# Scores in 64 by 64 tiles, an early fetch of sigmoid's table, and a rewritten order of all engines

## The chip, the cores and the metric

The kernel runs on one core of a Trainium2 chip. The time is device microseconds of one execution. Before the change three runs gave a median of 335.84 us (335.83 to 341.89). Inputs and weights start in device memory, and the output ends there.

## The reference

Three stages follow one another, all in float32, for a batch of 2 and 768 positions.

```python
# 1. linear attention with a decaying state: 8 heads, head_dim 48
for t in range(S):
    cur = einsum('bhd,bhe->bhde', u * k_t, v_t)
    y_t = einsum('bhd,bhde->bhe', r_t, state + cur)
    state = w_t[..., None] * state + einsum('bhd,bhe->bhde', k_t, v_t)
# x = y, heads side by side: [2, 768, 384]
# 2. gated MLP: d_ff 1024, gate over the positions
h = gelu_tanh(x @ w_in);  a, v = halves(h)
v_n = layernorm(v) * g_ln
x = x + (a * (einsum('ts,bsd->btd', w_sg, v_n) + b_sg)) @ w_out
# 3. channel mixing with a shift by one position
xk, xr = mu_k * x + (1 - mu_k) * x_prev, mu_r * x + (1 - mu_r) * x_prev
out = sigmoid(xr @ w_r) * (relu(xk @ w_k) ** 2 @ w_v)
```

## The kernel before, in words

The positions are cut into four blocks of 384, g = 0 to 3 (two for each batch entry). In the attention a block has three packs (L, q, D, j, g, d, K, f: loading and the decayed copies of r and k, VectorE work) and four units of two heads each, sixteen units in all. A unit's TensorE work is: T (turn: transposes of the keys), A (scores: keys against queries for three chunks of 128 positions), P (sums: two columns behind the scores, in the same PSUM tile), S and s (states and carry), J (inner: masked scores times values), N (inject) and I (outer: state times queries). VectorE's m (weigh, L359) masks the scores and n (now, L365) scales the values; ScalarE's k, x and O copy the turned keys, the states and the result. The fourth unit of each block is made of sixteen rows of each pack, which SyncE's queue moves with DMAs (6, and o for the way back, L396 and L397).

An operation on plain float32 operands shows as two weight loads and two matmuls in the trace; the stages behind the attention split each float32 number into a high and a low part (float32r) and add three products (`mm3`, L188 to L190). Weights come as raw words and are converted in chunks C0 to C38: l is the load, x, b, t VectorE's joining of the words, h the high part on ScalarE, o the low part on VectorE, r and q range checks on ScalarE.

The second stage runs by tiles v and u (both of `mm1`), M (`mm2`) and W (`mm_out`), the third by E (`mm_k`), R (`mm_r`) and Z (`mm_v`), with X, G, H (L490), Y, z and y as their elementwise steps and stores. E is a chain of five steps: nine matmuls on TensorE, Relu on ScalarE (L514), the square on VectorE (L516), the high part on ScalarE (L521), the low part on VectorE (L523). The tiles v, u, M, W, E and the idle matmuls share one PSUM pool of three buffers (`ps_d`); R and Z have another of five (`ps_e`). E's result kr has two buffers.

Nothing of the order is left to a scheduler: `ORDER` is a list of some 1250 tokens, each a step of the above with its number, and every engine and SyncE's DMA queue issue their own instructions in the order of this list. `E0.3` stands five times in it, once for each step of that chain. The token `e` is an idle matmul of 512 columns on zeros (L621). A step that is not ready stops its engine until it is.

The scores put the keys of head h (48 rows from row 64h) into the array with 128 columns, and write head h into the PSUM bank h:

Of the kernel before, what the change touches and what calls it, by code (L numbers as in the profile page):

```python
# [40 lines left out]
x3.2 e e T4 k4 A5 S4.0 K4 P5 s4.0 C2.b S4.1 x4.0 C2.t D5 C1.o j5 g5 J4 s4.1 C2.q x4.1 C2.h e e e N4 T5 I4 o3 o3 o3 X0.2.h X0.2.l X0.0.h f5 k5 C2.o K5
m5 C5.l v0.2 S5.0 s5.0 S5.1 J5 w6 63 L6 C5.x d5 X0.0.l n5 C3.x D6 C5.b C3.b x5.0 s5.1 C0.r x5.1 f4 X0.1.h X0.1.l C3.t j6 C5.t q6 64 65 w7 C4.l L7 v0.0
N5 T6 I5 O4 k6 S6.0 s6.0 S6.1 x6.0 v0.0 A7 P7 g6 n7 m7 s6.1 C3.h x6.1 f6 O5 C5.h C0.q v0.1 T7 d6 C5.o C4.x K6 k7 C5.r A6 P6 n6 m6 S7.0 s7.0 S7.1 J7
x7.0 s7.1 C5.q C4.b C4.t x7.1 C3.r C3.q C4.h v0.2 D7 C3.o C4.o N7 A8 P8 J6 T8 N6 u0.1 I7 q7 w8 C10.l C14.l q8 w9 n8 j7 g7 m8 K7 d7 I6 k8 v0.2 v0.0
S8.0 S8.1 O7 C14.h x8.0 C4.r J8 s8.1 S8.2 x8.1 f7 A9 P9 s8.2 L8 D8 j8 g8 n9 u0.1 v0.0 v0.0 x8.2 O6 K8 m9 d8 o7 o7 C8.l 66 67 o7 w10 q10 68 u0.3 N8
v0.1 v0.2 v0.1 T9 u0.2 k9 u0.0 I8 S9.0 S9.1 A10 X1.0.h x9.0 s9.1 S9.2 X1.2.h C10.h x9.1 u0.2 J9 P10 s9.2 X1.0.l C14.o C8.h X1.1.h f8 u0.3 O8 x9.2 m10
X1.2.l L9 D9 X1.1.l n10 C7.l C7.h C8.o v1.0 N9 v1.2 T10 A11 j9 v0.0 w11 q9 g9 d9 B L10 K9 v0.2 v0.1 v1.0 k10 S10.0 S10.1 v0.1 x10.0 v0.1 C10.o J10 P11
v0.2 n11 s10.1 S10.2 I9 x10.1 s10.2 C9.l C6.l f9 x10.2 v1.2 u0.0 O9 C7.o m11 C11.l q11 w12 v1.1 T11 N10 v1.2 v1.0 C6.h k11 C6.o D10 K10 j10 u1.1 u1.3
S11.0 S11.1 C11.h u1.3 x11.0 A12 P12 s11.1 S11.2 x11.1 v1.0 J11 s11.2 x11.2 u1.2 T12 N11 I10 I11 v1.1 69 C15.l L11 g10 m12 d10 C11.o n12 A13 v1.2 v1.0
v1.0 O10 k12 S12.0 s12.0 S12.1 v1.1 J12 x12.0 s12.1 P13 v1.2 u1.2 O11 x12.1 C9.h C9.o v1.1 C15.h v1.1 C12.l C12.h u1.1 o11 w13 C4.q D11 v1.1 v1.2  # L50
C15.o K11 C12.o n13 m13 C21.l o11 j11 g11 d11 N12 u1.0 u1.0 M0.3 M0.1 T13 k13 M0.2 A14 S13.0 s13.0 S13.1 J13 x13.0 s13.1 611 o11 X2.1.h C17.l w14
x13.1 P14 N13 T14 I13 I12 m14 n14 610 C26.l M0.2 A15 k14 C17.h C21.r C17.o O12 C21.q O13 S14.0 s14.0 S14.1 x14.0 J14 P15 s14.1 x14.1 X2.0.h M0.0 T15
C21.x m15 C16.l w15 C16.h C16.o X2.1.l M0.1 C26.x n15 C26.b C21.b M0.1 M0.0 C21.t M0.2 X2.2.h X2.2.l X2.0.l M0.3 C18.l C13.l N14 v2.1 k15 S15.0 s15.0
S15.1 C18.r x15.0 f11 J15 s15.1 N15 x15.1 I14 I15 C18.q f10 C13.h O15 v2.1 M0.3 C26.r O14 | C26.q C13.o C26.t v2.0 M1.2 C26.h C26.o M1.2 C20.l C20.r
C21.h v2.0 C19.l C21.o M0.0 v2.0 v2.2 M1.1 C20.q G0.3.h C20.x C20.b C20.t C18.x C18.b C18.t C18.h v2.0 v2.2 v2.2 v2.1 M1.1 M1.1 M1.0 M1.3 C18.o C19.x
C19.b M1.3 C19.r v2.1 C20.h v2.2 C19.t v2.0 v2.2 C19.h v2.1 C19.q M1.3 v2.0 M1.0 C19.o v2.2 M1.0 G0.2.h v2.1 u2.3 u2.0 u2.3 u2.1 u2.2 o15 C24.l G0.1.h
G0.0.h G0.1.l G0.0.l C20.o G0.2.l u2.0 u2.1 u2.2 G0.3.l W0.0 C24.x C24.b W0.0 M1.2 W0.1 W0.1 W0.2 C24.r C24.q C27.l o15 o15 C25.l C25.x X3.2.h C27.r
X3.0.h C27.q X3.0.l v3.0 C25.r X3.1.h C25.q v3.0 C25.b X3.2.l W0.2 X3.1.l C24.t v3.1 C24.h v3.0 C22.l C24.o C25.t C25.h C25.o C27.x C27.b C27.t C34.l
C23.l v3.2 u3.3 v3.0 v3.1 v3.1 u3.3 v3.2 u3.2 u3.0 u3.1 v3.2 u3.2 v3.0 v3.1 u3.0 v3.2 v3.0 C34.x C34.b C34.t v3.1 v3.1 G1.3.h v3.2 v3.2 C34.h G1.2.h
G1.2.l G1.1.h u3.1 G1.0.h C27.h C34.r C34.q C22.r C22.q M2.2 M2.2 C34.o C27.o M2.1 C23.x M2.1 C23.b C22.x G1.0.l M2.2 C22.b C22.t C23.t G1.3.l M3.3  # L60
# [838 lines left out]
```

## Time and profile before

| what | value |
|---|---|
| median of 3 runs | 335.84 us |
| profiled execution | 336.38 us, span 334.6 us |
| granted TensorE clock, mean | 0.996 |
| TensorE matmul busy | 323.1 us (97%), 2529 matmuls |
| VectorE busy | 232.0 us (69%) |
| ScalarE busy | 179.8 us (54%) |
| GpSimd busy | 35.4 us (11%) |

The profiled execution stands 0.54 us above the median of the runs, and its own time is 1.78 us longer than the span from its first to its last instruction. Busy time is an average over stages with different limits: the attention ends at about 122 us, the second stage runs mixed with it and to about 202 us, and the third from there to the end. A matmul's printed length overlaps that of the next, so that what a group of matmuls costs is read from its start to the start of the next group.

### The profile page before, as it was taken

The page shows a single profiled execution, that of the slowest core. Times are in us where ns is not written, and L with a number is a line of the kernel's source. Part 1 is how long each engine was busy: PE and PEld are TensorE (multiplying, and loading weights), DVE is VectorE, ACT ScalarE, POOL GpSimd, SP SyncE. Part 2 cuts the span into 40 slices and gives each one's busy share as a digit, 9 for nine tenths or more (in the row PEclk, how much of TensorE's full clock was granted, in tenths as well). Part 3 has the DMA queues.
Part 4 walks back from the last instruction along what each step waited for, and adds up shares of the span by engine and source line. Part 5 has one row for each costly group of instructions (what it writes and reads, how often), then busy time and mean ns, then how long its engine had stood idle before and what let it go on. Part 6 is the DMA issues. An engine that isn't in the chain of part 4 may idle for free.

```text
span 334.6 us, 6544 instructions
## 1 busy us (share of the span) xinstructions
PE 323.1 (97%) x2529; PEld 300.7 (90%) x2534; DVE 232.0 (69%) x427; ACT 179.8 (54%) x439; POOL 35.4 (11%) x78
## 2 busy tenths in 40 slices
...
GB/s 204 223 246 199 194 175 155 78 240 128 39 167 70 145 97 111 93 49 111 65 47 119 71 49 47 143 0 2 72 0 2 0 42 32 0 2 25 46 25 53
DMA packets 16500, 29.80 MB, mean 89 GB/s; under 512 B 2256, under 2 KB 12496, under 8 KB 16464
## 3 DMA queue, kind: packets, MB, share of 16 engines
...
## 4 chain that ended last, share of the span: by engine, by line
PE 77%; DVE 9%; ACT 5%; POOL 3%; DMA 2%; issue 2%; SPq 1%; ACTq 0%; POOLq 0%; DVEq 0%
PE po L542 11%; PE ps L188 5%; PE ps L190 5%; PE ps L189 5%; PE pk L188 4%; PE pk L190 4%; PE pk L189 4%; PE po L190 3%; PE po L189 3%; PE po L188 3%; PE pA L319 3%; PE py L385 2%; PE pu L188 2%; PE py L375 2%; PE pu L190 2%; PE pu L189 2%
## 5 line engine op out<-in xcount | busy, mean ns | idle before, releaser
L188 PE MATMUL pk<-xk_hi,wk_hi 128*128 128x384 f32 x96 | 32.5, 338 | 1.1 <-ACT kr L514 1.1
L188 PE MATMUL ps<-wsg,vn_hi 128*128 128x384 f32 x96 | 32.7, 340 | 0.0
L190 PE MATMUL ps<-wsg,vn_lo 128*128 128x384 f32 x96 | 32.5, 339 | 0.0
L190 PE MATMUL pk<-xk_hi,wk_lo 128*128 128x384 f32 x96 | 32.4, 337 | 0.0
L189 PE MATMUL ps<-wsg,vn_hi 128*128 128x384 f32 x96 | 32.4, 337 | 0.0
L189 PE MATMUL pk<-xk_lo,wk_hi 128*128 128x384 f32 x96 | 32.4, 337 | 0.0
L514 ACT ACTIVATE kr<-pk 128x384 f32<-128x384 f32 x32 | 15.5, 490 | 28.8 <-PE pk L190 14.6
L521 ACT CAST kk_hi<-kr 128x384 fp32r<-128x384 f32 x32 | 16.2, 512 | 19.3 <-DVE kr L516 19.3
L542 PE MATMUL po<-pl_win_hi,kk_hi 128*128 128x384 f32 x81 | 23.0, 337 | 0.0
L523 DVE TENSOR_TENSOR kk_lo<-kr,kk_hi 128x384 fp32r<-128x384 f32 x32 | 17.7, 555 | 6.9 <-ACT kk_hi L521 6.5
L359 DVE TENSOR_TENSOR am<-pA,c_sb 128x768 f32<-128x768 f32 x16 | 15.2, 951 | 8.9 <-PE pA L326 6.2
L516 DVE TENSOR_TENSOR kr<-kr 128x384 f32<-128x384 f32 x32 | 17.4, 555 | 4.4 <-ACT kr L514 4.3
L545 DVE TENSOR_TENSOR rr<-po,rr 128x384 f32<-128x384 f32 x12 | 6.6, 554 | 18.9 <-PE po L190 8.4
L188 PEld LDWEIGHTS pk<-xk_hi,wk_hi 128*128 128x128 f32 x96 | 18.0, 188 | 1.5 <-ACT kr L514 1.4
L542 PE MATMUL po<-pl_win_lo,kk_hi 128*128 128x384 f32 x63 | 18.4, 338 | 0.0
L190 PEld LDWEIGHTS ps<-wsg,vn_lo 128*128 128x128 f32 x96 | 18.0, 188 | 0.3 <-DVE vn_lo L446 0.2
L188 PEld LDWEIGHTS ps<-wsg,vn_hi 128*128 128x128 f32 x96 | 18.0, 188 | 0.3
L542 PE MATMUL po<-pl_win_hi,kk_lo 128*128 128x384 f32 x54 | 18.2, 338 | 0.0
L189 PEld LDWEIGHTS ps<-wsg,vn_hi 128*128 128x128 f32 x96 | 18.0, 188 | 0.1
L190 PEld LDWEIGHTS pk<-xk_hi,wk_lo 128*128 128x128 f32 x96 | 18.0, 188 | 0.0
L189 PEld LDWEIGHTS pk<-xk_lo,wk_hi 128*128 128x128 f32 x96 | 18.0, 188 | 0.0
L188 PE MATMUL pu<-xs_hi,win_hi 128*128 128x384 f32 x48 | 16.8, 350 | 0.1
...
## 6 DMA issues: line engine op xcount, KB each, us to landing
...
```

Source lines behind the costliest of these rows:

```text
L188: T.matmul(ps, lh, rh, start=(i == 0), stop=False)
L189: T.matmul(ps, lh, rl, start=False, stop=False)
L190: T.matmul(ps, ll, rh, start=False, stop=(i == n - 1))
L319: T.matmul(u.pA[:, h, c * C:(c + 1) * C], u.kinv[o:o + D, c, :], u.rp[o:o + D, c, :], start=True, stop=True)
L359: V.tensor_mul(u.am.rearrange("p h (c t) -> p h c t", c=NCB), u.pA[:, :, :TB].rearrange("p h (c t) -> p h c t", c=NCB), mask[:, None, None ...
L375: T.matmul(u.py[64 * h:64 * h + m, cs], u.vk[:, c, h * D:h * D + m], u.am[:, h, cs], start=(c == 0), stop=False)
L385: T.matmul(u.py[o:o + D, c * C:(c + 1) * C], u.state(c)[o:o + D, :], u.rp[o:o + D, c, :], start=False, stop=(c == NCB - 1))
L514: A.activation(kr, ps, AF.Relu)
L516: V.tensor_mul(kr, kr, kr)
L521: A.copy(hi, kr)
L523: V.tensor_sub(lo, kr, hi.bitcast(F32))
L542: T.matmul(pv[g][s], l, wv[i][r], start=st, stop=(i == KF - 1 and l is ll))
```

## The change

It makes three edits that act. A helper `minus` and the steps p and `rest` come with the diff too, but no token of the new order calls them, so they issue nothing.

```diff
         def scores(u):
             u.pA = ps_A.tile([P, 2, 512], F32, name=f"pA_{u.n}", tag="pA")
             for c in range(NCB):
-                for h in range(2):
+                for h, q in ((0, 0), (1, 64), (0, 64), (1, 0)):
                     o = 64 * h
-                    T.matmul(u.pA[:, h, c * C:(c + 1) * C], u.kinv[o:o + D, c, :], u.rp[o:o + D, c, :], start=True, stop=True)
+                    T.matmul(u.pA[q:q + 64, h, c * C:(c + 1) * C], u.kinv[o:o + D, c, q:q + 64], u.rp[o:o + D, c, :], start=True, stop=True)
...
+        elif kind == "F":
+            A.activation(warm, half, AF.Sigmoid)
...
-ORDER = """e L0 D0 j0 g0 q0 d0 e e e L1 D1 f0 e e e e e e e e e e e e e e e e e Q q1 w0 K0 j1 T0 g1 K1 d1 A0 k0 P0 S0.0 ...
+ORDER = """L0 D0 j0 e e e e e e e g0 f0 e L1 D1 q0 d0 j1 e e e e e e e e K0 g1 Q q1 L2 w0 q2 w1 A0 P0 T0 e e e e e e f1 k0 ...
```

The whole list is new, but its tokens are the old ones, with two differences: `e` stands 39 times instead of 44 and `F` is added. The parts that the prediction speaks of, old and new (in the second pair the tokens of SyncE's queue alone, in the third TensorE's alone):

```diff
-... N4 T5 I4 o3 o3 o3 X0.2.h X0.2.l X0.0.h f5 k5 C2.o K5 m5 C5.l v0.2 S5.0 s5.0 ...
+... X0.2.h X0.0.h N5 I4 I5 C2.b g5 d5 K5 C2.t T6 C2.h C5.r k6 w6 64 L6 w7 X0.2.l C1.o C2.o v0.2 S6.0 s6.0 ...
-... C2.l q4 q5 w4 L5 C3.l w5 o3 o3 o3 C5.l ...
+... L4 w4 q4 C2.l L5 C5.l o3 w5 q5 o3 63 o3 w6 ...
-... S1.2 A2 s1.2 P2 e T2 N1 I1 I0 S2.0 S2.1 A3 P3 ... N3 I3 I2 s3.2 e e e e T4 A5 ...
+... S1.2 I0 A2 s1.2 P2 e e T2 e e N1 S2.0 S2.1 J2 s2.1 S2.2 I1 A3 P3 ... N3 I3 A4 I2 s3.2 P4 ...
-... C28.x W2.1 E0.0 E0.1 E0.0 ... E0.1 E0.6 E0.2 E0.1 ... R0.0 R0.0 C28.q E0.6 E0.2 ... E0.2 H1 R0.2 R0.1 E0.3 ... C29.o E0.6 ... E0.5 W2.1 Z0.0 ...
+... W2.1 W2.1 Y0.1.1.a ... C36.o W2.0 E0.2 E0.0 C38.h E0.1 E0.5 ... E0.1 F E0.2 C31.b C31.t C29.x R0.0 R0.0 ... R0.2 ... E0.7 E0.7 E0.7 E0.6 H1 E0.6 ...
```

## Rows read from the trace of the kernel before

**Rows 1.** Busy time of each engine by stretch, us (x instructions), clock, DMA share, GB/s
```profile
20.00:30.00 10.00, 9.68 (x161) 8.24 (x162) 9.51 (x16) 6.83 (x19) 0.51 (x2) 1.00 0.93 301
37.00:60.00 23.00, 22.56 (x286) 18.75 (x284) 22.05 (x38) 16.63 (x46) 4.19 (x5) 1.00 0.58 167
...
122.00:200.00 78.00, 77.87 (x437) 75.49 (x433) 57.66 (x112) 52.58 (x126) 10.38 (x21) 1.00 0.26 82
...
220.00:317.00 97.00, 97.00 (x556) 96.85 (x555) 59.15 (x116) 39.52 (x89) 0.57 (x1) 1.00 0.05 19
...
sum 335.00, PE 323.08 PEld 300.71 DVE 232.04 ACT 179.85 POOL 35.42; mean PE 26.92 PEld 25.06 DVE 19.34 ACT 14.99 POOL 2.95
```

**Rows 2.** Timeline of TensorE's matmuls from 22 to 30 us: start, length, line, xcount
```profile
24.38 0.49 PE L379 MATMUL py<-c_sb,vg 128*112 128x128 f32 x3 [0.16 <-issue]
24.70 0.59 PE L621 MATMUL idle<-d1pat 128*128 128x512 bf16 x2
25.13 0.45 PE L308 MATMUL ptr<-c_sb,six 112*128 112x112 f32 x3
25.52 0.94 PE L319 MATMUL pA<-pk 48*128 48x128 f32 x12
26.39 0.32 PE L335 MATMUL pkv<-vk,kT 128*64 128x48 f32 x4
26.52 0.50 PE L326 MATMUL pA<-uu,pk 112*64 112x2 f32 x12
...
26.96 0.88 PE L375 MATMUL py<-am,vk 128*48 128x128 f32 x12
27.63 0.31 PE L346 MATMUL pkv<-sx,c_sb 112*48 112x48 f32 x4
...
28.46 0.64 PE L385 MATMUL py<-six,sx 48*48 48x128 f32 x8
28.94 0.60 PE L385 MATMUL py<-pk,sx 48*48 48x128 f32 x8
29.47 0.32 PE L346 MATMUL pkv<-sx,c_sb 112*64 112x48 f32 x4
```

**Rows 3.** Timeline around the first tile of the second stage, and SyncE's last share
```profile
33.68 0.59 SPq L397 DMA_DIRECT2D xT<-t  x1
...
36.11 0.93 ACT L416 CAST xs_hi<-xT 128x384 fp32r<-128x384 f32 x2 [1.52 <-issue]
36.66 0.56 DVE L418 TENSOR_TENSOR xs_lo<-xT,xs_hi 128x384 fp32r<-128x384 f32 x1 [1.30 <-ACT xs_hi L416]
...
36.67 0.50 PE L188 MATMUL pv<-win_hi,xs_hi 128*128 128x512 f32 x1 [0.91 <-ACT xs_hi L416]
```

**Rows 4.** Groups of VectorE instructions by line: xcount, busy us, mean ns, idle before
```profile
L359 DVE TENSOR_TENSOR am<-pA,c_sb 128x768 f32<-128x768 f32 x16 | 15.2, 951 | 8.9 <-PE pA L326 6.2 <-PE pkv L346 2.6
...
L259 DVE TENSOR_TENSOR pk<-pk,rk 128x768 f32<-128x768 f32 x12 | 11.5, 955 | 0.2
...
L365 DVE TENSOR_TENSOR vg<-pA,vk 128x288 f32<-128x288 f32 x16 | 7.2, 451 | 1.1 <-PE pA L326 1.1
...
L263 DVE TENSOR_TENSOR pk<-rk 128x384 f32<-128x384 f32 x12 | 6.5, 545 | 0.1
...
L169 DVE TENSOR_TENSOR win_lo<-winv_x,win_hi 128x512 fp32r<-128x512 f32 x3 | 2.0, 676 | 0.0
```

**Rows 5.** Timeline of ScalarE, VectorE and TensorE around 217 us
```profile
210.92 1.28 ACT L531 ACT_TABLE_LOAD   x1
...
214.13 0.56 DVE L516 TENSOR_TENSOR kr<-kr 128x384 f32<-128x384 f32 x1 [0.90 <-ACT kr L514]
214.61 1.35 DVE L490 TENSOR_TENSOR dx<-xT 128x1152 f32<-128x1152 f32 x1
...
217.01 0.49 ACT L514 ACTIVATE kr<-pk 128x384 f32<-128x384 f32 x1 [0.42 <-DVE kk_lo L523]
...
217.56 0.45 PE L188 MATMUL pk<-xk_hi,wk_hi 128*128 128x384 f32 x1 [1.05 <-ACT kr L514]
```

More of the change, by code (lines that the diff above doesn't have):

```diff
@@ L41 @@
[L41 to L60, printed above, removed]
@@ new lines @@
+x1.2 f2 O0 e e T2 e D3 n2 m2 j3 C0.x C0.b C0.t C1.t g3 e N1 k2 S2.0 S2.1 x2.0 J2 s2.1 S2.2 I1 A3 C1.q O1 P3 x2.1 s2.2 x2.2 f3 w3 q3 L4 m3 K3 D4 n3 j4
+d3 e e T3 N2 e e k3 S3.0 S3.1 C0.h x3.0 J3 s3.1 S3.2 N3 x3.1 I3 O3 A4 I2 s3.2 P4 x3.2 e T4 e e e k4 w4 q4 C2.l C2.r S4.0 s4.0 S4.1 L5 x4.0 g4 d4 K4 n4
+m4 A5 s4.1 P5 J4 C5.l o3 w5 q5 o3 D5 C0.o C2.x m5 n5 j5 f4 O2 x4.1 C1.h 63 o3 T5 k5 N4 e e S5.0 s5.0 S5.1 J5 x5.0 C2.q s5.1 x5.1 X0.2.h X0.0.h N5 I4
+I5 C2.b g5 d5 K5 C2.t T6 C2.h C5.r k6 w6 64 L6 w7 X0.2.l C1.o C2.o v0.2 S6.0 s6.0 S6.1 65 X0.0.l D6 C5.x j6 C5.b A7 C5.q X0.1.h x6.0 O4 C0.r s6.1 g6
@@ new lines @@
+O5 f6 x6.1 P7 C5.t C5.h v0.0 T7 n7 m7 v0.2 k7 A6 S7.0 P6 s7.0 S7.1 J7 X0.1.l q6 C3.l C3.x K6 C3.b n6 d6 C5.o C7.l C4.l C4.x w8 L7 q7 q8 m6 C3.t C4.b
+C4.t C0.q x7.0 s7.1 C7.h C3.r x7.1 v0.1 N7 T8 I7 A8 v0.0 f5 k8 C3.h O7 C3.q C4.h v0.0 C3.o D7 P8 S8.0 S8.1 J6 N6 o7 j7 C4.o n8 g7 m8 d7 u0.0 u0.3 I6
+A9 C4.r x8.0 v0.0 f7 s8.1 S8.2 C7.o K7 P9 m9 O6 v0.1 x8.1 J8 s8.2 v0.0 x8.2 u0.0 C8.l C9.l w10 o7 L8 C11.l L9 w9 o7 D8 K8 j8 g8 d8 n9 q9 B 68 66 N8
+u0.1 T9 u0.2 v0.1 v0.2 k9 C9.h S9.0 S9.1 C8.h X1.0.h X1.2.h x9.0 u0.2 C11.h C11.o X1.0.l C9.o X1.2.l I8 A10 P10 s9.1 S9.2 x9.1 J9 s9.2 v0.2 x9.2
@@ new lines @@
+o11 69 o11 X2.0.h C19.r v1.1 v1.2 D11 j11 g11 d11 m13 n13 K11 C15.o N12 M0.1 T13 M0.2 M0.2 A14 I12 X2.2.h X2.1.h X2.1.l C19.x C19.b C19.t C17.h C17.o
+k13 P14 S13.0 f11 s13.0 S13.1 J13 611 C13.l w14 w15 C12.l 610 C24.l m14 n14 M0.1 x13.0 s13.1 x13.1 O12 u1.3 f10 C19.q M0.0 N13 T14 I13 C13.h k14 A15
+P15 m15 X2.0.l M0.2 M0.1 C13.o S14.0 s14.0 S14.1 J14 x14.0 s14.1 C24.r x14.1 C12.h O13 N14 v2.0 T15 n15 M0.0 X2.2.l C24.x C24.b C24.t M0.3 M0.3 C18.l
+k15 S15.0 s15.0 S15.1 J15 x15.0 s15.1 x15.1 N15 I15 O15 C24.q C12.o I14 O14 C21.l | C19.h C24.h C21.r v2.2 v2.2 C21.q v2.0 C18.r C18.q C19.o C24.o
@@ new lines @@
+C21.x v2.1 M0.0 C18.x M0.3 C18.b C18.t C21.b C21.t M1.1 C26.l C20.l v2.2 C18.h C18.o M1.1 M1.2 C26.r v2.2 C26.x M1.1 M1.2 M1.3 M1.0 v2.1 G0.3.h C21.h
+C21.o v2.1 v2.0 C20.x C26.b C20.b C20.t C26.t M1.3 M1.3 C26.h v2.1 v2.0 v2.0 v2.2 v2.1 u2.2 v2.0 C20.h G0.3.l M1.0 M1.0 v2.1 u2.0 G0.1.h G0.0.h G0.0.l
+G0.1.l v2.2 C20.o u2.2 C26.q u2.1 u2.3 u2.0 u2.1 G0.2.h u2.3 C20.r o15 o15 o15 X3.2.h C20.q C34.l C27.l C27.r X3.1.h C25.l C27.q C25.r X3.0.h C25.q
+C27.x G0.2.l W0.2 W0.0 C27.b C27.t X3.1.l C26.o W0.2 v3.1 W0.1 X3.0.l X3.2.l v3.1 C25.x W0.1 C25.b v3.1 v3.2 v3.0 C27.h C27.o C25.t v3.1 v3.1 C34.x
@@ new lines @@
+C34.b W0.0 v3.2 v3.0 v3.0 v3.2 u3.3 u3.2 u3.3 u3.0 u3.1 u3.2 v3.0 C34.r C25.h C25.o C34.t v3.0 C23.l C22.l C28.l v3.2 C34.q u3.1 v3.2 v3.1 v3.0 C22.r
+G1.3.h G1.0.h G1.1.h v3.2 M2.3 M3.2 C22.x M1.2 C22.b C22.t C22.h u3.0 C22.q C34.h C22.o M3.2 M3.2 C34.o C28.x C28.b C28.t C28.h C28.o G1.0.l M2.1 M2.1
+C28.r C28.q G1.2.h C35.l C35.x M2.2 M2.2 C23.x C37.l M3.3 C35.r C35.b C35.t G1.2.l C35.h C35.q C35.o G1.3.l C38.l C23.b C23.t C23.h C38.r M2.2 M2.3
+G1.1.l M2.3 M2.0 C23.o M2.0 M2.0 M3.3 W1.0 W1.0 C37.x W1.2 W1.1 C38.x M2.1 G2.1.h G2.1.l C38.b G2.0.h G2.0.l W1.1 C37.b W1.2 C38.q C37.r C37.q G2.2.h
@@ new lines @@
+G2.2.l M3.0 M3.1 G2.3.h G2.3.l C37.t C23.r M3.0 H0 Y0.0.0.a C38.t Y0.0.2.a Y0.1.0.a M3.3 C31.l C29.l C36.l W2.2 M3.1 Y0.0.1.a C23.q Y0.1.0.b C31.r
+Y0.0.0.b Y0.0.1.b Y0.0.0.c W2.2 Y0.0.1.c C37.h C37.o Y0.1.2.a C31.q Y0.0.2.b Y0.0.2.c M3.0 M3.1 C36.x W2.0 W2.1 W2.1 Y0.1.1.a C36.b C36.t E0.0 C36.r
+Y0.1.2.b C36.q E0.0 C36.h Y0.1.1.b E0.0 Y0.1.0.c C36.o W2.0 E0.2 E0.0 C38.h E0.1 E0.5 Y0.1.1.c Y0.1.2.c C38.o E0.0 C31.x E0.1 F E0.2 C31.b C31.t C29.x
+R0.0 R0.0 C29.r E0.1 E0.1 G3.0.h R0.2 E0.2 C29.b C29.t E0.1 C29.h C29.o C30.l C32.l C33.l E0.3 E0.4 G3.1.h E0.3 E0.2 C31.h E0.3 C31.o R0.2 E0.3 E0.3
@@ new lines @@
+E0.5 C32.x C30.x C30.b C30.t G3.3.h C30.h E0.5 G3.3.l C30.o E0.2 E0.7 R0.1 R0.1 E0.6 C29.q C33.x C33.b C33.t E0.4 E0.4 C32.b C32.t C32.h C33.h E0.4
+C33.o E0.5 E0.5 C32.o E0.4 E0.6 E0.6 E0.7 E0.7 E0.7 E0.6 H1 E0.6 C33.r Y1.0.0.a Y1.0.0.b Y1.0.2.a E0.7 C33.q Y1.0.1.a Y1.1.1.a Y1.0.0.c Z0.0 Z0.1 Z0.2
+Z0.3 Z0.4 Z0.5 Z0.6 Z0.7 Y1.0.1.b Y1.0.2.b Y1.0.1.c Y1.0.2.c E1.0 E1.0 E1.0 Y1.1.0.a Y1.1.0.b E1.0 E1.0 z0.1 E1.2 E1.2 E1.1 E1.5 z0.2 E1.2 E1.1 E1.1
+E1.1 E1.2 Y1.1.2.a Y1.1.2.b Y1.1.2.c E1.2 E1.5 Y1.1.1.b G3.1.l E1.5 E1.5 E1.1 E1.6 E1.6 Y1.1.0.c z0.0 E1.5 E1.3 Z1.0 Z1.1 E1.4 E1.7 Z1.2 E1.3 E1.3
@@ new lines @@
+E1.3 G3.2.h G3.0.l E1.3 Z1.3 E1.6 Y1.1.1.c E1.6 E1.6 G3.2.l R1.0 W3.2 y0.1 y0.2 y0.0 H2 Y2.0.0.a Y2.0.1.a Y2.0.0.b Y2.0.1.b E1.4 E1.4 E1.4 Y2.0.1.c
+Y2.0.2.a Y2.0.0.c Y2.0.2.b Y2.0.2.c E2.0 E2.0 Y2.1.1.a E1.4 R1.1 Z1.4 Z1.5 Z1.6 R1.0 R1.1 E1.7 E1.7 Y2.1.0.a W3.2 E1.7 E1.7 Z1.7 R1.2 W3.0 E2.1 E2.0
+E2.0 Y2.1.0.b R1.2 Y2.1.1.b E2.0 z1.2 z1.1 Y2.1.2.a Y2.1.2.b E2.1 Y2.1.1.c Y2.1.0.c E2.3 E2.3 E2.3 Y2.1.2.c E2.3 E2.3 W3.1 W3.1 W3.0 E2.1 E2.1 E2.1
+E2.7 E2.4 E2.4 H3 E2.7 E2.7 E2.4 E2.7 E2.4 E2.4 R2.0 R2.2 E2.2 E2.2 E2.2 E2.2 E2.5 z1.0 E2.2 Y3.0.0.a Z2.0 E2.5 E2.7 E2.6 y1.1 y1.2 y1.0 E2.6 E2.6
@@ new lines @@
+Y3.0.2.a Y3.1.2.a Y3.0.1.a E2.5 E2.5 C30.r E2.5 R2.0 E2.6 Y3.0.0.b C30.q Y3.0.2.b Z2.1 Z2.2 Z2.3 Z2.4 Z2.5 Y3.0.0.c E2.6 Y3.0.2.c Y3.0.1.b Y3.0.1.c
+Y3.1.0.a R2.1 Z2.6 Z2.7 Y3.1.0.b E3.0 E3.0 E3.0 E3.2 E3.2 E3.2 Y3.1.1.a z2.0 E3.0 E3.2 R2.2 E3.2 E3.4 E3.0 E3.5 E3.1 Y3.1.1.b E3.4 E3.5 E3.5 E3.4
+Y3.1.0.c E3.4 R2.1 E3.4 E3.5 E3.6 E3.1 z2.2 Y3.1.1.c E3.5 E3.1 E3.1 E3.1 z2.1 E3.3 E3.7 y2.0 y2.1 y2.2 E3.6 Y3.1.2.b Y3.1.2.c R3.1 E3.3 E3.3 E3.3 E3.3
+R3.0 R3.2 E3.7 E3.6 E3.7 R3.0 E3.7 E3.7 C32.r R3.1 E3.6 E3.6 Z3.0 z3.0 Z3.1 z3.1 Z3.2 y3.0 y3.1 C32.q R3.2 z3.2 y3.2"""
@@ L141, in __init__ @@
             u.name, u.src, u.c0, u.n, u.single = f"{name}_{c0}", src, c0, n, src.dtype == F32
-            u.hi, u.lo = hi, lo
+            u.hi, u.lo, u.ps = hi, lo, None
         def load(u):
@@ L166, in high, with rest @@
             A.copy(u.hi(), u.x)
+        def rest(u):
+            u.ps = minus(u.x, u.hi())
         def low(u):
+            if u.ps is not None:
+                A.copy(u.lo(), u.ps)
+                return
             V.tensor_sub(u.lo(), u.x, u.hi().bitcast(F32))
@@ L182, in fused_kernel, with minus @@
     sized = {}
+    def minus(x, hi):
+        n = x.free_size() if hasattr(x, "free_size") else int(np.prod(x.shape[1:]))
+        ps = ps_d.tile([P, 512], F32, name=f"rest{len(rests)}", tag="d")[:, :n]
+        if len(x.shape) == 3:
+            ps = ps.rearrange("p (k t) -> p k t", k=x.shape[1])
+        rests.append(ps)
+        T.matmul(ps, eye, x, start=True, stop=False)
+        T.matmul(ps, less, hi, start=False, stop=True)
+        return ps
+    rests = []
     def mm3(ps, terms):
@@ L416, in xsplit @@
             A.copy(xs[0][:, :, ts], x)
+        elif step == "p":
+            xrest[c] = minus(x, xs[0][:, :, ts])
+        elif g == 0 and c in xrest:
+            A.copy(xs[1][:, :, ts], xrest[c])
         else:
             V.tensor_sub(xs[1][:, :, ts], x, xs[0][:, :, ts].bitcast(F32))
-    vn = {}
+    xrest, vn = {}, {}
     def mm1_v(g, s):
```

30 lines of the change are left out of this document (7 added, 23 removed).

## The prediction, made before the run

> **What bounds the kernel now.** I read the busy time by stretch first. In the stretch from 122 to 200 us and in that from 220 to 317 us TensorE is busy without a break [rows 1], and there only less TensorE work could shorten the run; the change leaves these products as they are. So whatever it gains or loses lies in three places: the first 37 us, where VectorE is the full engine (9.51 of 10 us, and still 22.05 of 23 us up to 60 us [rows 1]) and TensorE fills holes with idle matmuls; the attention work that is mixed with the second stage up to 122 us, where TensorE's own time per step counts; and a single hole near 217 us. The timeline of TensorE then gives the price of a step (start to start), and the timelines around 36 and 217 us say which wait ended last there.
>
> **The scores, 16 times.** A pass of 128 float32 columns over the undivided array takes (24.70 - 24.38) / 3 = 0.107 us [rows 2]. The inner products need 0.67 us for twelve such passes (26.96 to 27.63), the outer ones 1.01 us for sixteen (28.46 to 29.47) [rows 2], so both run in pairs: column halves of the array side by side in the first, diagonal quarters in the second. The scores of before take 0.87 us for twelve (25.52 to 26.39) [rows 2]: six pairs are 0.64 us, and 0.23 us are entry and exit, against 1.01 - 8 x 0.107 = 0.15 us for the outer products and 0.03 us for the inner ones, whose neighbours divide the array as they do. The new scores have 24 passes, six for each quarter. Nothing in this trace runs four quarters at once. If they do, a unit costs 6 x 0.107 + 0.15 = 0.79 us, a gain of 0.08; if only two go side by side, 12 x 0.107 + 0.15 = 1.43 us, a loss of 0.56. Over 16 units that is from 1.3 us less to 9.0 us more. I take four at once: column halves and row halves are each shown to be independent, and the data that the inner products stream (all rows, two column halves) is as much per pass as four quarters ask for. Ten of the sixteen units (A6 to A15) come after the first tile of the second stage, where TensorE has no holes; the other six lie among idle matmuls. So I count 10 x 0.08 = **0.8 us less**.
>
> **Divisions of the array.** Scores now divide it as the outer products do, and the new list puts them side by side (I0 A2, I1 A3, I3 A4 I2). Counted along TensorE's tokens the division changes 66 times instead of 73. One side of a change is 0.15 / 2 = 0.07 us by the outer products and 0.23 / 2 = 0.11 us by the old scores; seven are 0.5 to 0.8 us, **0.4 us less** where they count.
>
> **The start.** The first tile v0.2 waited for xs_hi (36.67 us, idle 0.91 us), which waited for the shares o3 of unit 3: the last of six DMAs was issued at 33.68 us, behind the load w5 on SyncE's queue, and xs_hi started at 36.11 us; VectorE stood 1.30 us for it [rows 3]. In the new list the first o3 is ahead of w5, q5 and 63 are between the others (they wait for products that come before I3), and X0.2.h stands behind unit 5's states. Then VectorE sets the start: ahead of X0.2.l it now also has d5, K5, m5 and n5 and no longer C1.o, 0.96 + 0.55 + 0.95 + 0.45 - 0.68 = 2.23 us [rows 4]. Of this 1.30 us fill its old wait, so xs_lo and with it v0.2 come about 0.9 us later. But by then TensorE has also done the rest of unit 5 and a turn: five states and carries at 0.13 (26.39 to 26.52), 0.67 inner, 0.32 inject, twelve outer passes 0.76 and a turn 0.39 (25.13 to 25.52), together 2.8 us [rows 2], in time that went to idle matmuls. The net is **1.9 us less**, with ends at 0.9 us more (if what was moved costs nothing later anyway) and 2.8 us less. The five idle matmuls taken out are worth nothing by themselves; they fill waits.
>
> **The hole at 217 us.** TensorE stood 1.05 us before a tile of E [rows 5]. It waited for a PSUM buffer, that for the Relu at 217.01 us, which had waited for a kr buffer, freed by VectorE's low part of E0.6. VectorE was late twice: 0.90 us idle until the Relu that came behind the table load of 1.28 us on ScalarE, and then 1.35 us for H1 ahead of that low part [rows 5]. All this bites because only two PSUM buffers went round: W2.1 gave its own back only behind all of E0. The new list changes all three: W2.1's addition stands ahead of E0.0's square, H1 behind E0.7's square, and F loads the table ahead of E0.2's Relu. F costs ScalarE 1.28 us and, for its one column, up to a Relu's 0.49 us [rows 5]; queued behind it are E0.2's Relu and R0.0's sigmoid, and E0.4 waits for that Relu's buffer. TensorE has R0.0, R0.2 and E0.3 to do in between, 27 passes of 97.00 / 556 = 0.174 us [rows 1] or 4.7 us, R on the other PSUM pool. So F is hidden; without that cover it would cost up to 1.8 us. Late next would be E0.6, which needs E0.5's Relu, and this the low part of E0.3. **1.1 us less**, ends 0 and 1.3.
>
> **The sum.** 0.8 + 0.4 + 1.9 + 1.1 = 4.2 us. The profiled execution took 336.4 us, so 332.2 us; it was 0.5 us over the median of the runs, which alone would give 331.6. I predict **332.0 us**.
>
> **Rivals.** (1) The quarters take turns. For it: four at once is shown nowhere, and the two column halves of a head read the same 48 rows. Against it: the inner products' column halves also share all their rows, and their weight loads and passes still hide in each other (0.67 us for twelve [rows 2]). It decides as soon as a unit's scores take over 1.1 us, in the ten units where TensorE has no holes: 0.56 x 10 = 5.6 us more in place of 0.8 us less, so 332.0 + 6.4 = 338.4 us, slower than before; 341 us if the six early units show it too.
>
> The Trainium skill has a rule for this in "TensorE: Matmul & The Clock Gate", Part 3: a weight load overlaps running matmuls only when it goes to other rows of the array. By that rule the halves (0,0) and (0,64) would load in turn, and the sum would be that of rival 1. The inner products of this trace speak against it.
>
> (2) The start gains nothing: unit 5's work is late on ScalarE or SyncE's queue, so that TensorE waits there as before. For it: six steps on three queues have to come in time before X0.2.h; against it: VectorE alone was full there [rows 1]. Then 332.0 + 1.9 = 333.9 us; with the full 0.9 us of delay and a hole in E as before, 336 us. (3) More is gained: the attention up to 60 us, where VectorE is nearly full, also runs smoother because VectorE has unit 5 behind it when the second stage begins. Another 2 to 3 us, 329 us. (4) F does not do what it says: if the load still comes where sigmoid is first used, or stands in the way of E0.2's Relu, the hole stays, 333.1 us.
>
> **How the numbers follow.** Forecast (with rival 4) 55%, rival 2 20%, rival 3 10%, rival 1 15%. The range 329.0 to 338.5 us holds the forecast with its bounds, rival 2, most of rival 3 and the nearer half of rival 1; the likeliest case alone has 330 to 334 us. Two per cent (6.7 us), about what a measurement of this kernel can tell from no change, puts the limits at 329.1 and 342.6 us: faster 0.08 (the far side of rival 3), slower 0.05 (rival 1 at its full price, or with a start that is late), the rest within.
>
> **What would show it.** Scores: the start-to-start time of a unit's 24 passes between 0.75 and 0.85 us is right, 1.4 us is rival 1. Start: v0.2 at about 37.5 us with unit 5 done before it; at 36 us with unit 5 still to do, or after 39 us, the step is wrong. E: no idle time of TensorE between 195 and 225 us, and a table load of 1.28 us before the first R. Between 225 and 317 us TensorE must stay full; a new hole there, where H2 and H3 have also moved, would make the forecast wrong in a way that I have not priced.

## The result, and the profile after

| | before | after |
|---|---|---|
| median of the runs, us | 335.98 (335.09 to 341.89, 9 runs) | 332.41 (331.62 to 334.06, 9 runs) |
| profiled execution, us | 336.38 | 332.00 |
| its span, us | 334.6 | 330.2 |

The ratio is 0.9877 (95% interval 0.9851 to 0.9903): 1.2% faster, which is inside the two per cent called no change, but its interval lies clear of 1. The forecast was 332.0 us.

The busy time by stretch of the kernel after, with the same columns as in [rows 1]:

```profile
30.00:37.00 7.00, 7.00 (x120) 5.74 (x120) 6.93 (x12) 4.56 (x14) 0.45 (x1) 1.00 0.56 143
...
122.00:200.00 78.00, 76.57 (x429) 74.90 (x428) 58.21 (x112) 49.17 (x113) 10.52 (x23) 1.00 0.24 75
200.00:220.00 20.00, 19.99 (x115) 19.67 (x114) 17.69 (x38) 13.20 (x30) 1.13 (x2) 1.00 0.19 60
220.00:317.00 97.00, 97.00 (x553) 97.00 (x552) 58.49 (x111) 40.87 (x92) 0.00 (x0) 1.00 0.05 19
```

Two rows answer to the forecast at once. From 200 to 220 us TensorE is now busy for 19.99 of 20 us: the hole near 217 us [rows 5] is gone. From 220 to 317 us it is full, as before. One row does not fit: from 122 to 200 us, where [rows 1] has 77.87 us busy of 78, there are 76.57. A stall has come in that nobody had asked for.

TensorE's longest waits of the kernel after (us in all, times, longest) name it. The first row lies ahead of the first matmul and the third at the end of the kernel:

```profile
PE idle L644 <- POOL lim_tanh L119: 1.4, 1, 1.4
PE pu L207 <- ACT v L453: 1.4, 1, 1.4
PE pf L676 <- DVE fl L673: 0.8, 1, 0.8
PE pA L338 <- issue: 0.5, 1, 0.5
```

**Where the 4.4 us of the profiled runs came from.** I set a mark at the start of the first tile of the second stage, v0.2. It starts at 36.67 us before [rows 3] and at 36.66 us after. From there to the last product (the second matmul of pf, starting at 330.66 and 326.24 us) it is 293.99 us before and 289.58 after, so the whole gain lies behind the mark. Giving each of TensorE's matmuls the time from its own start to the next one's start, and adding these up by kind, the attention work behind the mark falls from 43.30 to 37.92 us, 5.4 less. All other products take 250.69 us before and 251.66 after, 1.0 more. A product's loss is here its time beyond a steady 0.175 us for 384 columns, or 0.23 us for 512. The hole near 217 us was a loss of 1.22, and the largest loss at E after the change is 0.17, at 203 us; ahead of one tile u the loss is 0.30 before (at 159 us) and 1.59 after (at 152 us).

The last part of this stretch, from the first product of E to pf, has the same 722 matmuls in every kernel here. I call it the third stage. It starts at 202.21 us before and at 198.31 after, and takes 128.45 and 127.93 us. So closing the hole of 1.22 us shortened the stage by 0.5 us only; the rest went in losses of under 0.1 us each, spread over the stage.

**The scores.** TensorE's timeline of the kernel after, from 25 to 31 us, columns as in [rows 2]:

```profile
26.37 0.88 PE L338 MATMUL pA<-pk 48*64 48x128 f32 x24
27.07 0.60 PE L404 MATMUL py<-pk,sx 48*48 48x128 f32 x8
...
29.93 0.89 PE L338 MATMUL pA<-pk 48*64 48x128 f32 x24
30.75 0.31 PE L365 MATMUL pkv<-sx,c_sb 112*64 112x48 f32 x4
```

The reader is to take differences of starts: 24 passes take 30.75 - 29.93 = 0.82 us between other work, and 27.07 - 26.37 = 0.70 us between two halves of the outer products, which divide the array in the same way. The old form, twelve passes, took 0.87 us [rows 2].

**The start.** The timeline around v0.2 after the change, which answers to [rows 3]:

```profile
33.21 0.32 PE L354 MATMUL pkv<-vk,kT 128*64 128x48 f32 x4
...
33.99 0.58 SPq L416 DMA_DIRECT2D xT<-t  x1
...
35.94 0.68 DVE L163 SCALAR_TENSOR_TENSOR winv_x<-winv_raw,winv_x 128x512 int32<-128x512 int32 x1
36.05 0.93 ACT L435 CAST xs_hi<-xT 128x384 fp32r<-128x384 f32 x2 [1.04 <-DMA xT<-t]
...
36.38 0.51 PE L327 MATMUL ptr<-c_sb,pk 112*128 112x112 f32 x3
36.60 0.56 DVE L441 TENSOR_TENSOR xs_lo<-xT,xs_hi 128x384 fp32r<-128x384 f32 x1
36.66 0.47 PE L207 MATMUL pv<-win_hi,xs_hi 128*128 128x512 f32 x1
```

ScalarE still stands 1.04 us for the last share's DMA, but neither VectorE nor TensorE stands for it: VectorE comes to its low part (36.60 us) straight from a conversion step, and TensorE works 7.00 of 7.00 us between 30 and 37 us, on unit 5 from 33.21 us and on the next unit's turn at 36.38. In the kernel before, this work of unit 5 stood behind the mark:

```profile
39.09 0.32 PE L335 MATMUL pkv<-vk,kT 128*64 128x48 f32 x4
...
40.34 0.50 PE L188 MATMUL pv<-win_hi,xs_hi 128*128 128x512 f32 x1
...
42.60 0.49 PE L379 MATMUL py<-c_sb,vg 128*112 128x128 f32 x3
42.93 0.45 PE L308 MATMUL ptr<-c_sb,pk 112*128 112x112 f32 x3
43.31 0.42 PE L385 MATMUL py<-pk,sl 48*48 48x128 f32 x4
...
44.10 0.32 PE L335 MATMUL pkv<-vk,kT 128*64 128x48 f32 x4
```

States, carries and inner take 40.34 - 39.09 = 1.25 us, inject, turn and outer 44.10 - 42.60 = 1.50 us: 2.75 us in all.

**The table load.** ScalarE after the change:

```profile
203.70 1.28 ACT L651 ACT_TABLE_LOAD   x1
205.00 0.20 ACT L651 ACTIVATE warm<-half 128x1 f32<-128x1 f32 x1
205.11 0.47 ACT L537 ACTIVATE kr<-pk 128x384 f32<-128x384 f32 x1
```

F does what it says: the load is ahead of a Relu instead of behind one, and F's own column adds 205.11 - 205.00 = 0.11 us.

**The new stall.** Three timelines of the kernel after around 152 us, GpSimd's, ScalarE's and TensorE's (the bracket is the engine's idle time before the instruction, and what ended it):

```profile
149.16 0.58 POOL L506 COPY xT<-xT 128x1 f32<-128x1 f32 x1 [3.98 <-DVE xT L504]
149.71 0.67 POOL L458 TENSOR_SCALAR ln<-ln 128x1 f32<-128x1 f32 x1
150.47 0.86 POOL L459 TENSOR_TENSOR ln<-ln,half 128x1 f32<-128x1 f32 x1
151.43 0.47 POOL L460 TENSOR_SCALAR ln<-ln 128x1 f32<-128x1 f32 x1
```

```profile
147.69 0.72 ACT L457 ACTIVATE vj<-v,ln 128x512 bf16<-128x512 f32 x1
148.32 0.18 ACT L457 ACTIVATION_READ_ACCUMULATOR vj<-v,ln 128x1 f32 x1
...
151.93 0.81 ACT L462 ACTIVATE v<-v,ln 128x512 f32<-128x512 f32 x1 [2.92 <-POOL ln L460]
...
153.30 0.59 ACT L453 ACTIVATE v<-pv 128x512 f32<-128x512 f32 x1
```

```profile
154.04 0.45 PE L207 MATMUL pu<-xs_hi,win_hi 128*128 128x384 f32 x1 [1.43 <-ACT v L453]
```

Read it from the bottom. TensorE wants a PSUM buffer that the Gelu at 153.30 us frees. That Gelu is queued on ScalarE behind v3.1's normalization at 151.93 us, which has waited 2.92 us for three operations on one column each by GpSimd (lines 458 to 460). ScalarE's sum of squares for them was there at 148.50 us (148.32 + 0.18), but GpSimd's queue had W0.1's copy of one column first (line 506), and that waits for VectorE's addition, which waits for W0.1's last product: GpSimd stood 3.98 us. In the old list both tokens of W0.1 come long before the square of v3.1; in the new list W0.1's second token stands between v3.1's second and third.

### The profile page after: what moved, and what is told of

Read it like the earlier page. It is cut to its first block, busy times and chain, and to the rows that moved or that the text cites. A ratio compares the mean times of both kernels' runs of the same rounds, so it can differ in the third digit from the quotient of the medians.

```text
span 330.2 us, 6938 instructions
## 1 busy us (share of the span) xinstructions
PE 321.7 (97%) x2721; PEld 299.3 (91%) x2721; DVE 232.7 (70%) x427; ACT 180.9 (55%) x440; POOL 28.6 (9%) x78
## 4 chain that ended last, share of the span: by engine, by line
PE 91%; DVE 3%; DMA 2%; ACT 1%; POOL 1%; issue 1%; SPq 0%; ACTq 0%; DVEq 0%
PE po L565 12%; PE pk L207 5%; PE ps L207 5%; PE pk L208 5%; PE pk L209 5%; PE ps L209 5%; PE ps L208 5%; PE po L209 4%; PE po L208 4%; PE po L207 4%; PE pA L338 3%; PE pu L207 3%; PE py L394 3%; PE py L404 3%; PE pu L209 3%; PE pu L208 3%
## 5 line engine op out<-in xcount | busy, mean ns | idle before, releaser
L208 PE MATMUL po<-ga_lo,wout_hi 128*128 128x384 f32 x48 | 16.2, 337 | 0.0
```

The source lines that it names most:

```text
L208: T.matmul(ps, lh, rl, start=False, stop=False)
```

## The experiments

What each kernel is measured by: the median and ratio against the kernel before, in runs taken together with it, and the stretch from the mark v0.2 to pf in its profile. The stretch leaves out the start, which moves: v0.2 comes at 35.83 to 36.67 us in four profiles with the old list, and 37.58 in a fifth, at 36.64 to 38.01 in seven with the new one (idle matmuls and scores as in the change, or the old scores).

The stretch has noise of its own. With the old list and the old scores, from v0.2 to the first product of E, where none of the edits below acts, four profiles have 165.53 us (the kernel before), 166.42, 164.61 and 165.04. So a difference of a single old-list profile under 1.8 us is not read from the whole stretch. The third stage is much steadier: 127.90 to 127.96 us in all nine profiles with the new list. Edits in E are read from it.

**The change again.** No edit.

> The changed kernel once more, beside its variants: all theories expect 332.4 us, 1.2% under the kernel before, and the hole of TensorE of 1.4 us near 153 us again, since it belongs to the order of the queues.

Measured: 332.56 us (332.02 to 333.24), ratio 0.9899 (0.9869 to 0.9928); v0.2 at 37.06 us, from there 289.23 us. The wait for v L453 is there again with 1.4 us. So two profiles of the same kernel with the new list differ by 0.35 us in this stretch, and effects below that are not read from it.

**The new list with the old scores.**

```diff
-for h, q in ((0, 0), (1, 64), (0, 64), (1, 0)):
+for h in range(2):
     o = 64 * h
-    T.matmul(u.pA[q:q + 64, h, ...], u.kinv[o:o + D, c, q:q + 64], ...)
+    T.matmul(u.pA[:, h, ...], u.kinv[o:o + D, c, :], ...)
```

> The new list with the old scores (64 rows by 128 columns). Theory: the tile form is a small part of the gain. A unit's scores take 0.87 us instead of 0.82 us, and the eight or so units of the saturated part that stand beside outer products lose the common division of the array, some 0.1 us each: 0.5 + 0.8 = 1.3 us slower than the changed kernel (0.7 to 2.0), still 2 to 3 us faster than the kernel before. Rival: the tile form carries the gain, and the time is back at 335.5 us or more. Second rival: it carries nothing, and the time stays at 332.4 us.

Measured: 333.17 us (333.06 to 333.52), ratio 0.9915 (0.9886 to 0.9943), against 332.56 for the change beside it: 0.6 us. From v0.2 it is 290.13 us, 0.6 to 0.9 more than the two profiles of the change. The kernel's timeline beside the outer products:

```profile
26.80 0.94 PE L338 MATMUL pA<-pk 48*128 48x128 f32 x12
27.67 0.64 PE L404 MATMUL py<-pk,sx 48*48 48x128 f32 x8
```

27.67 - 26.80 is 0.87 us, what the old kernel paid [rows 2], where the new tiles need 0.70 in that place. What follows: the tiles with their fewer divisions are worth 0.6 us, just under the 0.7 to 2.0 that were expected and half of the 1.2 us that the prediction gave to both.

**The old list with the new scores.** The reverse edit, in the kernel before.

> The kernel before with the new scores alone, in the old list. Theory: a unit's scores take 0.82 us instead of 0.87 us start to start, which counts in the ten units behind the first tile of the second stage: 0.5 us, and 0.1 to 0.2 us for the two places where the old list already has them beside outer products. The time falls by 0.3 to 0.9 us. Rival: quarters in an old list, among other neighbours, take turns, over 1.1 us for a unit and 3 us or more slower.

Measured: 338.09 us, ratio 1.0029 (0.9993 to 1.0064): no gain; missed. The scores' time behind the mark does fall, from 9.93 to 9.25 us, but TensorE's timeline has two holes that the kernel before has not, and VectorE, whose low part the first one waits for, had itself stood 2.01 us for a DMA:

```profile
95.53 0.96 DVE L248 TENSOR_TENSOR_SCAN pk<-wt,d1pat 128x387 f32<-128x387 f32 x1 [2.01 <-DMA wt<-in_wp_dram]
...
97.13 0.44 PE L190 MATMUL ps<-wsg,vn_lo 128*128 128x384 f32 x1 [0.82 <-DVE vn_lo L446]
...
110.23 1.01 PE L319 MATMUL pA<-six 48*64 48x128 f32 x24 [0.87 <-DMA wk_raw<-in_w_k_dram]
```

Both waits go back to a DMA. A likely reading is that TensorE, sooner at these places, met data that did not come sooner. That this cancels the gain is not shown: other waits of the kernel before are missing here, and a gain of 0.7 us lies inside the noise of the old list's profiles.

**Every pass of the scores twice.**

```diff
-for h, q in ((0, 0), (1, 64), (0, 64), (1, 0)):
+for h, q in ((0, 0), (1, 64), (0, 64), (1, 0)) * 2:
```

> The changed kernel with every unit's scores computed twice into the same tile (48 passes a unit). Theory: quarters run four at once, so that 24 more passes cost 6 x 0.107 = 0.64 us a unit; ten units stand where TensorE is full, so 6.4 us more, up to 8 us with the early ones, and the start-to-start time of a unit's scores is 1.46 us. Rival: they run two at once, 1.28 us a unit and 12.8 us more.

Measured: 341.86 us (341.01 to 343.09), ratio 1.013 (1.0067 to 1.0193). The kernel's timeline, one unit between other work:

```profile
47.82 1.54 PE L338 MATMUL pA<-pk 48*64 48x128 f32 x48
49.29 0.32 PE L354 MATMUL pkv<-vk,kT 128*64 128x48 f32 x4
```

48 passes take 1.47 us where 24 take 0.82: 24 more cost 0.65 us, which is six passes of 0.107 us [rows 2], one after another, in each of four quarters. That is the direct price of the tile form, free of entry and exit, and it leaves no room for quarters that take turns in pairs (1.28 us). From v0.2 the run is 294.88 us, 5.3 more, a little under the ten units' 6.5; v0.2 itself came at 40.31 us, so the early units, which I had put among idle matmuls, were not free when doubled. In time it is 2.3 to 2.6% more than the change by the ratios, some 8 us, at the upper end of the 6.4 to 8 expected.

**The new list without F.**

```diff
-... E0.1 F E0.2 ...
+... E0.1 E0.2 ...
```

> The new list without the operation F, so that sigmoid's table is loaded where sigmoid is first used. Theory: the hole in E had more than one cause, and the new list also gives back the third buffer early and puts H1 behind the squares; the load then falls on ScalarE at about 206 us while TensorE has R tiles and buffers to spare, so that no hole of over 0.3 us returns and the time stays within 0.5 us. Rival: the fetch is what closed the hole, and without it 1.0 to 1.3 us come back between 205 and 220 us.

Measured: 333.14 us, ratio 0.9909 (0.9878 to 0.9939); from v0.2 289.63 us, as with F. The load goes back in front of the first sigmoid:

```profile
206.75 1.28 ACT L554 ACT_TABLE_LOAD   x1
```

and no wait of TensorE in E comes back; the third stage takes 127.92 us, as with F. The 0.6 us more of the median (333.14 against 332.56) are not in E: v0.2 came at 37.75 us in this profile. In the new list F carries nothing.

**The old list with F alone**, ahead of E0.6's Relu.

```diff
-... C31.x E0.0 Y0.1.1.b E0.1 E0.6 ...
+... C31.x E0.0 Y0.1.1.b E0.1 F E0.6 ...
```

> The kernel before with F alone, ahead of the Relu of E0.6. Theory: the load moves into time in which ScalarE waited for VectorE (1.9 us up to 209.9 us), VectorE loses the 0.90 us in which it waited for a Relu, and the hole of 1.05 us shrinks to 0.1 to 0.4 us, not to nothing, since H1 and the two buffers stay: 0.6 to 1.0 us faster. Rival: H1 and the missing buffer set it, and the hole stays over 0.8 us.

Measured: 337.47 us, ratio 0.9985 (0.9953 to 1.0017); from v0.2 294.98 us, 1.0 more than before, of which 0.9 lie ahead of E, where nothing was edited. The third stage takes 128.56 us against 128.45. Missed: the hole stays. VectorE, ScalarE and the wait that ends the hole, in this kernel:

```profile
207.82 1.28 ACT L628 ACT_TABLE_LOAD   x1
...
209.75 0.56 DVE L523 TENSOR_TENSOR kk_lo<-kr,kk_hi 128x384 fp32r<-128x384 f32 x1 [1.21 <-ACT kk_hi L521]
...
218.91 0.49 ACT L514 ACTIVATE kr<-pk 128x384 f32<-128x384 f32 x1 [0.86 <-DVE kk_lo L523]
```

The load stands ahead of another high part, VectorE waits 1.21 us for that, and the Relu of before waits again for the low part. Moving the load only moves who is late.

**The old list with W2.1's addition early.** The buffer comes back ahead of E0.0's square.

```diff
-... E0.1 E0.0 Y0.1.2.c C31.x E0.0 ... E0.5 W2.1 Z0.0 ...
+... E0.1 E0.0 Y0.1.2.c C31.x W2.1 E0.0 ... E0.5 Z0.0 ...
```

> The kernel before with one step moved: the addition of W2.1, which gives back a PSUM buffer, stands ahead of E0.0's square instead of behind all of E0. Theory: the hole of 1.05 us at 217 us needs a buffer that goes round among two; with the third one back in time E0.7 takes it and the hole is gone (under 0.3 us), without F and with H1 where it was: 0.7 to 1.1 us faster from the first tile of the second stage to the end. Rival: VectorE's lateness shifts the hole to the next tile of E, and it stays over 0.8 us.

Measured: 336.71 us, ratio 1.0011 (0.9982 to 1.0041). TensorE's waits in this kernel have no row for pk any more (it had 1.1 us for kr before). But a new one has come behind E, at the first tiles of Z. ScalarE's and TensorE's timelines:

```profile
222.15 0.49 ACT L514 ACTIVATE kr<-pk 128x384 f32<-128x384 f32 x1 [2.30 <-DVE kk_lo L523]
...
222.42 0.34 PE L542 MATMUL po<-pl_win_lo,kk_lo 128*128 128x384 f32 x1
223.09 0.62 PE L542 MATMUL po<-pl_win_hi,kk_hi 128*128 128x384 f32 x2 [0.34 <-ACT kk_hi L521]
```

Here a product starts 223.09 - 222.42 = 0.67 us after the one before it, 0.50 us over the pace, and the next three steps lose 0.4 us more. The last Relu of E0 had stood 2.30 us for VectorE's low part, which frees a kr buffer. So the third buffer takes the hole out of E and the time does not fall: the wait comes back behind E, by way of kr's two buffers, and the third stage takes 128.57 us against 128.45. From v0.2 it is 293.18 us, 0.8 less than before, but that lies ahead of E (0.9 less), in the part that the edit leaves alone.

**The old list with H1 late**, behind E0.6's low part.

```diff
-... E0.2 H1 R0.2 ... G3.3.h E0.3 Y1.0.0.a ...
+... E0.2 R0.2 ... G3.3.h E0.3 H1 Y1.0.0.a ...
```

> The kernel before with H1 (1.35 us on VectorE) moved behind the low part of E0.6. Theory: that low part can then come only when the conversion ahead of it has its high part from ScalarE, at about 215.4 us, so it starts near 215.9 instead of 216.3 us, and the hole shrinks by some 0.4 us to about 0.6 us. Rival: H1 alone made the hole, and it goes altogether.

Measured: 336.47 us, ratio 1.0011 (0.998 to 1.0042); from v0.2 293.85 us, and the third stage 128.81 us, 0.4 longer than before. Missed: nothing is gained. The wait of TensorE for kr in this kernel:

```profile
PE pk L188 <- ACT kr L514: 1.1, 2, 0.6
```

The one wait of 1.05 us has become two that add up to 1.1. The likely reason is that H1 costs VectorE its 1.35 us [rows 5] wherever it stands, and the next low part pays.

**The new list with v3.1's third step ahead of W0.1's second.**

```diff
-... v3.1 C25.x W0.1 C25.b v3.1 v3.2 ...
+... v3.1 v3.1 C25.x W0.1 C25.b v3.2 ...
```

> The new list with one step moved: the third step of tile v3.1 (square, then three small GpSimd operations of the layer norm) stands ahead of W0.1's second step (addition, then a copy of one column on GpSimd). Theory: TensorE's hole of 1.4 us at 153 us comes from GpSimd's queue, where the small operations stood behind a copy that waits for W0.1's matmuls (GpSimd started it at 149.2 us, the square was done at 148.3 us), and ScalarE waited 2.9 us for them. Moved, the hole shrinks to under 0.4 us and the time by 1.0 to 1.6 us. Rival: the PSUM buffers set it, since u3.3 waits for the gelu of v3.2 in any case: the hole stays over 1.0 us and the time with it.

Measured: 331.77 us (330.6 to 335.0), ratio 0.989 (0.9844 to 0.9936); from v0.2 287.76 us, 1.5 to 1.8 less than the two profiles of the change. GpSimd in this kernel:

```profile
149.63 0.22 POOL L458 TENSOR_SCALAR ln<-ln 128x1 f32<-128x1 f32 x1 [3.40 <-ACT vj L457]
...
151.34 0.66 POOL L506 COPY xT<-xT 128x1 f32<-128x1 f32 x1
```

The first small operation now waits for ScalarE's square and for nothing else, and the copy, which nobody was waiting for, is behind. TensorE's wait for v is gone. The median fell less than the stretch because v0.2 came at 38.01 us in the profile, the latest of all, so it was run again:

> The changed kernel with the small GpSimd operations of v3.1 ahead of W0.1's copy, once more, since its first profile had a first tile 1.3 us later than the changed kernel's from the same steps ahead of it. Theory: from the first tile of the second stage to the last matmul it takes 287.8 us again, 1.7 us less than the changed kernel, and its median is 330.5 to 332 us, the fastest of all. Rival: the lateness of the start belongs to the moved step, and the time is the changed kernel's 332.5 us.

Measured: 330.79 us (330.45 to 332.6), ratio 0.9853 (0.9816 to 0.989), v0.2 at 37.20 us and from there 287.95 us. Both medians with this list, 331.77 and 330.79, are under both of the change, 332.41 and 332.56, and its ratios lie clear of 1: it is faster than the kernel before. The step over the change is 0.8 us in time (331.77 against 332.56 in runs taken together), which these runs do not resolve, since the ranges and the ratios' intervals overlap; behind the mark it is 1.3 to 1.8 us in each pair of profiles, clear of the 0.35 us between the change's own two.

**The new list with the last share one place earlier on SyncE's queue.**

```diff
-... 63 o3 T5 ...
+... o3 63 T5 ...
```

> The changed kernel with the last share o3 issued ahead of the move 63 on SyncE's queue, 1.1 us earlier. Theory: at 36.66 us three things end together, the share that xs_hi waits for, VectorE's work and TensorE's turn T6 (TensorE was busy without a break from 30 to 37 us); one of them earlier changes nothing, and v0.2 and the time stay within 0.3 us. Rival: xs_hi waited 1.04 us for the share's DMA, so the start follows the queue, v0.2 comes 0.6 to 1.0 us earlier and the time falls by as much.

Measured: 333.77 us against 337.25 for the kernel before beside it, ratio 0.9878 (0.9829 to 0.9927); v0.2 at 36.64 us, from there 289.59 us. ScalarE's high part and VectorE's low part:

```profile
35.47 0.93 ACT L435 CAST xs_hi<-xT 128x384 fp32r<-128x384 f32 x2 [0.48 <-ACT sx L373]
...
36.53 0.55 DVE L441 TENSOR_TENSOR xs_lo<-xT,xs_hi 128x384 fp32r<-128x384 f32 x1
```

The high part comes 0.6 us earlier than in the change and waits for no DMA; VectorE's low part, again without idle time ahead of it, and v0.2 stay where they were. So the last share does not set the start here.

**The new list without its 39 idle matmuls.**

> The changed kernel without any of its 39 idle matmuls. Theory for the five that the change took out: they fill waits of TensorE that last until VectorE is ready, so that even all 39 fewer move nothing as long as the granted clock stays at its full level; then v0.2 comes within 0.5 us of the changed kernel. Rival: without them the granted clock falls to its lower level in the first 30 us, passes of 0.107 us take 0.213 us, v0.2 comes 3 us later or more and the time is 335 us or more.

Measured: 336.49 us, ratio 0.9999 (0.9965 to 1.0033), as the rival had it; v0.2 at 40.12 us, from there 289.97 us. Nearly all that is lost is lost before the mark. The kernel's timeline:

```profile
13.31 1.56 PE L338 MATMUL pA<-pk 48*64 48x128 f32 x24
14.80 0.45 PE L365 MATMUL pkv<-sx,c_sb 112*64 112x48 f32 x4
...
20.18 0.97 PE L338 MATMUL pA<-pk 48*64 48x128 f32 x22
21.08 0.32 PE L365 MATMUL pkv<-sx,c_sb 112*64 112x48 f32 x4
```

TensorE was busy for 2.56 of the first 10 us in this run and for 8.29 in the change. At 13.31 us 24 passes of the scores take 1.49 us, at 20.18 us 22 passes take 0.90; in the change 24 passes take 0.82 us already at 7.45 us. A pass at 13 us takes nearly twice as long, which fits the lower of the clock's two levels (1.2 GHz) and, by 20 us, the upper one (2.4 GHz). Between the two TensorE was busy for most of the time (9.47 us of those from 10 to 20). The level is inferred from the passes: the column of the granted clock by stretch prints 1.00 for the whole of this run. No run takes out only the five idle matmuls that the change left out.

## Why the prediction came out, step by step

The number was right. Of its terms the start had the right size, scores and divisions and the hole came to about half of theirs. A stall that no term had took 1.3 us back, and attention work that no term had gave about 1.9. That these errors nearly cancel, so that 332.0 us meets 332.41, is luck.

**Scores and divisions (forecast 0.8 + 0.4).** The mechanism was right. Four quarters do run at once: six passes' worth for 24, by the doubled scores 0.65 us against the 6 x 0.107 = 0.64 of the prediction. The unit came out at 0.82 us by itself, against 0.79, and at 0.70 us between the outer products. The first means that entry and exit cost more than the outer products' 0.15 us, 0.18; the second that they are saved where neighbours divide the array alike. Swapping the tiles back cost 0.6 us of time, not 1.2. The step was mis-sized by half. By the starts, scores and outer products together are 1.3 to 1.6 us shorter than with the old tiles, but the states next to them grew by about 0.4 and 0.3 was lost in the stream of projections.

Rival 1 has fallen. The Trainium skill's rule in "TensorE: Matmul & The Clock Gate", Part 3, by which a weight load hides behind running matmuls only when it goes to other rows of the array, would have the two column halves of one head load in turn. No run here agrees: 0.82 us for 24 passes, 1.47 for 48.

**The start (forecast 1.9: 2.8 of work done earlier, 0.9 of delay).** Both parts hold over the profiles, neither of them in one. The work of unit 5 that disappears from behind the mark adds up to 2.75 us. In the profile of the change v0.2 was not late at all, so all of it counted; but over seven profiles with the new list v0.2 starts at 37.2 us in the mean, against 36.5 us over the five with the old, 0.7 us later. The reason given for the delay, that VectorE sets the start, fits five of these seven profiles: VectorE goes to the low part without idle time. In the other two it stood 0.18 and 0.57 us for ScalarE's high part, and that for the share's DMA. TensorE has next to no hole there either, so that its own work, VectorE's and the share end almost together, and no run tells which of them sets the start. Rival 2 has fallen with the 7.00 busy us of 7.00 ahead of v0.2.

**The hole in E (forecast 1.1).** The hole went as forecast: a loss of 1.22 us became 0.17. The time it was to give did not come in full: the third stage is 0.5 us shorter, in all nine profiles with the new list. Of the three causes that the prediction named, none carries it alone. The load's place does nothing (taken out of the new list, the hole does not return; put into the old one, it stays), H1 moved alone splits the hole in two, and the buffer that W2.1 gives back early moves it behind E. In the prediction's words, "all this bites because only two PSUM buffers went round": with the third the chain bites a little later, by way of kr's two buffers. No run puts the early buffer and the late H1 together into the old list, so which other step of the new list keeps the wait from coming back stays open. Rival 4 tied the hole to F too, and falls with that: F did what it says and was not needed.

**What the forecast did not have.** The list moved W0.1's second token to between two tokens of v3.1. The prediction read SyncE's queue around v0.2, and VectorE's and ScalarE's around 217 us; it looked for unpriced holes behind 220 us, where H2 and H3 moved, and found TensorE full there. GpSimd's queue at 152 us was not read, because GpSimd has so little work (28.6 of 330.2 us) and nothing there was on the path. It cost 1.3 us (1.59 against 0.30), and the two profiles without it are 1.3 to 1.8 us shorter behind the mark.

Against it stands a gain that was not forecast either: the attention work behind the mark fell by 5.4 us, 2.75 of it unit 5's and about 0.8 the scores' and divisions'. Of the rest 1.0 is one wait of TensorE for kT, 1.01 us at 76.77 us before: the five profiles with the old list have it with 0.61 to 1.24 us, those with the new list have none over 0.1. For the last 0.9 us, spread over many steps of the attention and no more than the noise of the old list's profiles, no run singles out a cause. It is the direction of rival 3 (2 to 3 us), in part; but the wait for kT lies behind the 60 us that rival 3 speaks of.

In sum, of the 4.4 us between the two profiles: unit 5 about 2.7, scores and divisions about 0.8, the wait for kT 1.0, other attention work 0.9, the third stage 0.5, less 1.3 for the new stall and 0.2 for the other projections. The medians differ by 3.57 us, 0.8 less; the later v0.2, 0.7 us in the mean of the profiles, would explain that, but the runs without a profile do not show where v0.2 starts.
